# Softmax reciprocals of a fused attention and MoE kernel: 28 of 32 loads issued by SyncE, 14 transposes two steps sooner

## The chip, the cores and the metric

The kernel runs on one NeuronCore of a Trainium2 chip. The core has TensorE (PE, with its weight loads shown apart as PEld), VectorE (DVE), ScalarE (ACT), GpSimd (POOL) and SyncE (SP, which only issues DMAs). Each engine works through its own instructions in order, and engines wait for each other by semaphores. The metric is the device time of one execution in microseconds. The kernel before took 644.96 us, the median of 3 runs (644.65 to 645.30).

## The reference

Three stages in float32. First an attention in which a query sees only the keys of its own cluster, then two feed-forward stages:

```python
mask = q_assign[:, :, :, None] == k_assign[:, :, None, :]      # argmax over 16 centroids
scores = np.where(mask, scale * q @ k.T, -1e9)
scores = scores - np.max(scores, axis=-1, keepdims=True)
attn = np.exp(scores)
attn = attn / (np.sum(attn, axis=-1, keepdims=True) + 1e-09)   # the reciprocals of this case
x = attn @ v                                                   # [2, 8, 768, 64] -> [1536, 512]
x = leaky_relu(x @ w_in) @ w_out                               # 512 -> 2048 -> 512
out = x + gate * expert(x)   where x @ w_skip > 0, one of 8 experts per token, 512 -> 1024 -> 512
```

The inputs are 2 batches of 8 heads with 768 tokens and 64 values a head.

## The kernel before, in words

The attention is a written-out sequence of 96 steps. Two heads make a pair; there are 8 pairs (p = 0 to 7) of 12 steps each (r = 0 to 11). Six steps make a group g (0 to 15): three tiles of 128 queries for two heads. In step s TensorE computes the scores of one query tile against all 768 keys (tile `sps`), VectorE takes the row maximum (`st`), ScalarE takes the exponential with its row sum (`pr`, `sm`). Three steps later (LAG = 3) TensorE transposes the 128x768 exponentials in six pieces (`tps`) and ScalarE copies them to SBUF in two halves (`pt`). In every second step TensorE multiplies them with the values (`avps`, 8 matmuls). At the end of a group ScalarE copies the sum out (`xr`) and GpSimd multiplies it with the reciprocals (`rb`) and splits it into two parts for the next stage (`xh`, `xl`).

The reciprocals take their own way. With rf the step within the six that follow a group: at rf 0 and 1 VectorE adds 1e-9 to the six row sums and inverts them (`rc`); at rf 4 `recip_rows` has TensorE transpose `rc` into PSUM (`rcps`) and ScalarE copy six rows out (`rrow`); at rf 5 SyncE writes them to DRAM (`recip_scratch`); one step later (rf 0 of the next six) GpSimd issues `recip_load`, two DMAs that spread them over 128 partitions (`rb`); at the next rf 2 GpSimd multiplies.

Beside this each pair is prepared during the steps of the pair before. A table (`plan`) names step and slot of each part: slot "a0" comes before the transposes of a step, "pb" at its end. The preparation uses one PSUM buffer, tag "M", of which there is a single one (`ps_m`, bufs=1). For pairs 3 to 7 it holds in turn four transposed pieces of q and k (`rawps`: TensorE at the end of steps 5, 6, 7 and 8, ScalarE reads each in slot "a0" of the step after, tile `raw`), then the centroid scores (`asps`, step 9, read in step 10), their transposes (`scps`, step 10) and in step 2 of the next pair the masks (`ohps`). `rcps` is a tile of the same buffer. In every fourth step ScalarE also starts the conversion of a piece of 64-bit weights (`cvu`).

What a step appends stands in this order in the program: scores, weight conversion, slot "a0", transposes and their copies, `recip_rows`, values, exponential, end of group, `recip_load`, `recip`, slots "d" and "pb". The functions that matter are `recip_rows` (L404), `recip_load` (L411), `raw_act` (L187) and the step loop (L688 on). SyncE issues nearly all other transfers of the stage in the order written: copies between halves (`UA`, `UB`, `VA`, `VB`), masks (`mk`), values, weights (`stg`).

Of the kernel before, what the change touches and what calls it, by code (L numbers as in the profile page):

```python
# [20 lines left out]
def _f(ap):  # L21
    return ap.bitcast(F32)
# [3 lines left out]
def kernel(  # L26
# [14 lines left out]
    nc = tc.nc  # L41
# [17 lines left out]
    def pool(name, side=None, **kw):  # L59
        return tc.alloc_tile_pool(name=name, side=side, bufs=1, reuse_waits="tile", **kw)  # L60
# [8 lines left out]
    def ps_s(name):  # L69
        return psum.tile([P, 2, 512], F32, tag="S", name=name, bufs=2)  # L70
# [281 lines left out]
    NSTEP = B * NPAIR * 12  # L352
# [5 lines left out]
    def where(s):  # L358
        p, r = divmod(s, 12)
        half, r = divmod(r, 6)  # L360
        j, h = divmod(r, 2)
        return p, half, j, h

    def st_scores(s):
        p, half, j, h = where(s)
        U, V = (uv_t[p][h], uv_t[p][2 + h])
        qs = slice((3 * half + j) * P, (3 * half + j + 1) * P)
        ps = ps_s("sps")
        for (t, n), first in (((U, 80), True), ((V, P), False)):
            for kh in range(2):  # L370
                nc.tensor.matmul(ps[:, kh, 0:HS], lhsT=t[0:n, 0, qs], rhs=t[0:n, 1, kh * HS:(kh + 1) * HS],  # L371
                                 start=first, stop=not first)
        st = att.tile([P, 1], F32, tag="st", name="st", bufs=7)
        nc.vector.tensor_reduce(out=st[:, 0:1], in_=ps[:, :, 0:HS], axis=AX.XY, op=ALU.max, negate=True)  # L374
        pr = att.tile([P, 2, HS], F32R, tag="pr", name="pr", bufs=4)
        pr = _f(pr)
        p_t[s] = pr, st
        s_t[s] = ps
# [13 lines left out]
    rc_t, rrow_t = {}, {}  # L392
# [9 lines left out]
    rscr = nc.dram_tensor("recip_scratch", (NSTEP // 6, 6, P), F32, kind="Internal").ap()  # L402

    def recip_rows(g):  # L404
        ps = (ps_t if g == NSTEP // 6 - 1 else ps_m)([P, P], "rcps")
        nc.tensor.transpose(ps, rcs[g % 2], ident)
        row = att.tile([6, P], F32, tag="rrow", name="rrow", bufs=2)
        nc.scalar.activation(out=row, in_=ps[0:6, :], func=AF.Copy)
        rrow_t[g] = row

    def recip_load(g):  # L411
        rb = att.tile([P, HS], F32, tag="rb", name="rb", bufs=1)
        for h in range(2):
            nc.gpsimd.dma_start(rb[64 * h:64 * h + 64, :], rscr[g, 3 * h:3 * h + 3, :].rearrange("j q -> (j q)").partition_broadcast(64))
        rrow_t[g] = rb

    t_t = {}

    def st_transpose(s):
        p, half, j, h = where(s)  # L420
        if j == 0:
            pt_t[p, half, h] = att.tile([P, NT, 3, P], F32, tag=f"pt{h}", name=f"pt{h}", bufs=2)
        pr, _ = p_t.pop(s)
        t_t[s] = []
        for kh in range(2):
            ps = ps_t([P, 3, P], "tps")
            for t in range(3):
                nc.tensor.transpose(ps[:, t, :], pr[:, kh, t * P:(t + 1) * P], ident)  # L428
            t_t[s].append(ps)

    def st_evac(s):
        p, half, j, h = where(s)
        pt = pt_t[p, half, h]
        for kh in range(2):
            nc.scalar.activation(out=pt[:, 3 * kh:3 * kh + 3, j, :], in_=t_t[s][kh], func=AF.Copy)  # L435
        t_t.pop(s)

    def st_av(g, kt):
        p, half = divmod(g, 2)
        if kt == 0:  # L440
            av_t[g] = (ps_m if g == NSTEP // 6 - 1 else ps_a)([P, HS], "avps")
        for h in range(2):
            nc.tensor.matmul(av_t[g][64 * h:64 * h + 64, :], lhsT=vnat[p][:, h, kt, :],  # L443
                             rhs=pt_t[p, half, h][:, kt].rearrange("p j c -> p (j c)"),
                             start=(kt == 0), stop=(kt == NT - 1))
# [3 lines left out]
    def av_evac(g):  # L449
        xr_t[g] = att.tile([P, HS], F32, tag="xr", name="xr")  # L450
        nc.scalar.activation(out=xr_t[g], in_=av_t.pop(g), func=AF.Copy)
# [98 lines left out]
    def load_piece(c, a):  # L550
        if wsp[0] is None or a % 2:
            t = ring_a.tile([P, 512, 2], U32, tag="stg", name="stg", bufs=2)
        else:
            t = wsp[0].tile([P, 512, 2], U32, tag="stg2", name="stg2", bufs=2)
        g, wo = divmod(c, 2)
        if wo == 0:
            src = wi_u[a * P:(a + 1) * P, g * 1024:(g + 1) * 1024]
        else:
            src = wo_u[g * 512 + a * P:g * 512 + (a + 1) * P, :]
        nc.sync.dma_start(t, src.rearrange("p (f two) -> p f two", two=2))  # L560
        stage[c, a] = t
# [3 lines left out]
    def convert_op(c, a, i):  # L565
        st = stage[c, a]
        w0, w1_ = st[:, :, 0], st[:, :, 1]
        V = nc.vector
        if i == 0:
            cv[c, a] = [ring_a.tile([P, 512], U32, tag=n, name=n, bufs=2) for n in ("cvu", "cvt")]  # L570
        u, t = cv[c, a]
        if i == 0:
            nc.scalar.activation(out=_f(u), in_=_f(w1_), func=AF.Abs)
        elif i == 1:
            V.tensor_scalar(out=_f(u), in0=_f(u), scalar1=2.0 ** -15, scalar2=None, op0=ALU.max)
        elif i == 2:
            V.tensor_scalar(out=t, in0=u, scalar1=3, scalar2=0x3FFFFFF8, op0=ALU.logical_shift_left,
                            op1=ALU.bitwise_and)
        elif i == 3:
            V.scalar_tensor_tensor(out=t, in0=w1_, scalar=0xC0000000, in1=t, op0=ALU.bitwise_and, op1=ALU.bitwise_or)  # L580
        else:
            direct = not NDIR <= 4 * c + a < NPC
            if direct and (a == 0 or c not in chunks):
                chunks[c] = alloc_chunk(c)
            o = chunks[c][:, a, :].bitcast(U32) if direct else t
            V.scalar_tensor_tensor(out=o, in0=w0, scalar=29, in1=t, op0=ALU.logical_shift_right, op1=ALU.bitwise_or)
            stage.pop((c, a))
            if direct:
                cv.pop((c, a))
# [23 lines left out]
    def preps(p, r, slot):  # L613
        prep(p + 1, r, slot)
        if r >= 4:
            prep(p + 2, r - 12, slot)
# [3 lines left out]
    def conv_step(s, late):  # L620
        n = 2 * s + late - CONV0
        if s == 6 and not late:
            load_piece(0, 0)
            load_piece(0, 1)
        m, r = divmod(n, CPER)
        if 0 <= m < NPC:
            c, a = divmod(m, 4)
            if r < 5:
                convert_op(c, a, r)
            elif r == 6:  # L630
                if m >= NDIR:
                    nc.sync.dma_start(wf32[c - NDIR // 4, :, a, :], _f(cv.pop((c, a))[1]))
                if m + 2 < NPC:
                    load_piece(*divmod(m + 2, 4))
# [54 lines left out]
    for s in range(NSTEP + 12 + LAG):  # L689
        p, r = divmod(s, 12)  # L690
        if s < NSTEP:
            st_scores(s)
        conv_step(s, 0)
        preps(p, r, "a0")
        preps(p, r, "pa")
        if 0 <= s - LAG < NSTEP:
            st_transpose(s - LAG)
            st_evac(s - LAG)
        gf, rf = divmod(s, 6)
        if 0 < gf <= NSTEP // 6:  # L700
            if rf == 4:
                recip_rows(gf - 1)
            elif rf == 5:
                nc.sync.dma_start(rscr[gf - 1], rrow_t.pop(gf - 1))
        g, kt = divmod(s - 6 - LAG, 6)
        if 0 <= g < NSTEP // 6 and kt % 2:
            st_av(g, kt - 1)
            st_av(g, kt)
        if s < NSTEP:
            st_exp(s)  # L710
        if 0 <= g < NSTEP // 6 and kt == NT - 1:
            av_evac(g)
            av_split(g)
        if 0 <= g < NSTEP // 6 and kt == 3:
            recip_load(g)
        if 0 < gf <= NSTEP // 6 and rf < 2:
            recip(gf - 1, rf)
        preps(p, r, "d")
        preps(p, r, "pb")
        if r == 10 and p + 1 < NP:  # L720
            load_v(p + 1)
        conv_step(s, 1)
        if s == NSTEP:
            att_a.release()
            rt = pool("rt", "left")
            ring_b[0] = pool("ring_b", "left")
            wip[0] = pool("wi", "left")
            for c in range(NDIR // 4, NPC // 4):
                load_f32(c)
            load_next(2)  # L730
        if s == NSTEP + 4:
            for i in range(3):
                split_i(i)
# [891 lines left out]
```

## Time and profile before

| what | value |
|---|---|
| median of 3 runs | 644.96 us (644.65 to 645.30) |
| profiled execution | 644.19 us, its span 642.5 us |
| TensorE busy in the span | 624.0 us, 97% |
| ScalarE, VectorE, GpSimd busy | 65%, 75%, 26% |
| the 96 attention steps | from 18.6 us on; the last values end at 252.6 us |

Times in rows are microseconds from the span's start. In the chain of waits a row gives start, length and what the time went to; consecutive rows join without gaps, so the start of one is the end of the one before. A row of instructions in order of time ends with the idle time of the engine before it and its releaser, in brackets. Matmuls overlap: their ends are modelled.

### The profile page before, as it was taken

Reading aid. Unit: us, or ns where it says so; the run is one execution under the profiler, and the core shown is the slowest. Engines: PE = TensorE matmul, PEld = TensorE weight load, DVE = VectorE, ACT = ScalarE, POOL = GpSimd, SP = SyncE. Lnnn points to the kernel's source line nnn. Section 1 sums busy time; section 2 is a strip of 40 time slices with the busy share of each in tenths; the row PEclk is TensorE's granted clock in tenths of the full one; section 3 lists DMA queues with packets and bytes.
Section 4 is the critical chain, followed back from the end, with each engine's and each line's share of the span. In section 5 each row is a group of like instructions: output and inputs, shape, how many; then the busy total and the mean of one; then the engine's idle time right before and its main releaser. Section 6 shows DMA issues by size and latency. Waiting matters only on the chain.

```text
span 642.5 us, 10035 instructions
## 1 busy us (share of the span) xinstructions
PE 624.0 (97%) x3505; PEld 484.2 (75%) x3505; DVE 484.7 (75%) x893; ACT 417.0 (65%) x817; POOL 164.4 (26%) x215
## 2 busy tenths in 40 slices
PE   5999999999999999999999999999999999999994
PEld 3777777677777775888888888878888778688874
DVE  6757868777878754988865888868887748999961
ACT  5798898988888885655454444435445446688860
POOL 3333647463746333400000000000000125005211
PEclk9999999999999999999999999999999999999998
DMA  7766566578766508132014301008421739999930
GB/s 189 193 180 169 138 153 190 150 197 199 200 186 162 174 31 318 67 119 91 23 36 146 100 33 34 33 2 301 178 94 66 267 137 318 372 363 350 369 135 28
DMA packets 66246, 104.26 MB, mean 162 GB/s; under 512 B 27994, under 2 KB 32060, under 8 KB 65810
## 3 DMA queue, kind: packets, MB, share of 16 engines
q1 hardware_dynamic: 62914, 95.36, 47.5%
q0 software_dynamic: 3280, 8.24, 3.9%
q8 instruction: 28, 0.46, 0.3%
q14 instruction: 24, 0.20, 0.1%
HBM read 77.45 MB, written 12.72 MB: 140 GB/s over the span
## 4 chain that ended last, share of the span: by engine, by line
PE 91%; DVE 3%; ACT 2%; DMA 2%; SPq 1%; issue 1%; POOL 0%; POOLq 0%
PE ups L669 20%; PE acc L775 19%; PE sps L371 10%; PE avps L443 10%; PE tps L428 9%; PE hps L1316 7%; PE yps L1347 7%; PE rawps L179 1%; PE hT L1328 1%; PE acc L1208 1%; PE asps L232 1%; ACT pr L389 1%; DMA stg<-in_moe_w_in_dram 1%; DMA first<-in_k_dram 1%; PE scps L244 1%
## 5 line engine op out<-in xcount | busy, mean ns | idle before, releaser
L374 DVE TENSOR_REDUCE st<-sps 128x1 f32<-128x768 f32 x96 | 91.5, 954 | 49.9 <-PE sps L371 49.1
L435 ACT ACTIVATE pt<-tps 128x384 f32<-128x384 f32 x192 | 85.4, 508 | 17.6 <-PE tps L428 16.4
L389 ACT ACTIVATE pr<-sps,st 128x768 f32<-128x768 f32 x96 | 88.0, 917 | 11.5 <-DVE st L374 11.4
L428 PE MATMUL tps<-ident,pr 128*128 128x128 f32 x576 | 79.0, 273 | 0.5 <-ACT pt L435 0.5
L669 PE MATMUL ups<-xh,whii 128*128 128x512 f32 x192 | 74.9, 390 | 0.0
L669 PE MATMUL ups<-xh,wloi 128*128 128x512 f32 x192 | 74.7, 389 | 0.0
L669 PE MATMUL ups<-xl,whii 128*128 128x512 f32 x192 | 74.7, 389 | 0.0
L428 PEld LDWEIGHTS tps<-ident,pr 128*128 128x128 f32 x576 | 67.9, 140 | 5.6 <-ACT pt L435 1.6
L443 PE MATMUL avps<-pt,vnat 128*64 128x384 f32 x384 | 72.1, 498 | 0.0
L775 PE MATMUL acc<-whio,gh 128*128 128x512 f32 x183 | 72.1, 394 | 0.0
L775 PE MATMUL acc<-whio,gl 128*128 128x512 f32 x183 | 71.3, 389 | 0.0
L775 PE MATMUL acc<-wloo,gh 128*128 128x512 f32 x183 | 71.2, 389 | 0.0
L760 ACT ACTIVATE gh<-g 128x512 fp32r<-128x512 f32 x48 | 30.4, 632 | 47.5 <-DVE g L759 47.5
L758 ACT ACTIVATE lk<-ups 128x512 f32<-128x512 f32 x48 | 28.5, 595 | 48.8 <-PE ups L669 43.4
L762 DVE TENSOR_TENSOR gl<-g,gh 128x512 fp32r<-128x512 f32 x48 | 33.2, 691 | 25.2 <-ACT gh L760 25.2
L1048 POOL DMA_INDIRECT xe<-x_scratch,eix x1 | 1.2, 1165 | 189.8 <-DVE eix L1047 189.8
L881 DVE SCALAR_TENSOR_TENSOR ohe<-x,x2Ts 128x512 f32<-128x512 f32 x63 | 43.4, 689 | 1.5
L443 PEld LDWEIGHTS avps<-pt,vnat 128*64 128x64 f32 x384 | 23.4, 136 | 25.5 <-issue 25.1
L759 DVE TENSOR_TENSOR g<-ups,lk 128x512 f32<-128x512 f32 x48 | 33.0, 688 | 12.7 <-ACT lk L758 12.1
L669 PEld LDWEIGHTS ups<-xh,whii 128*128 128x128 f32 x192 | 36.0, 188 | 8.0 <-issue 0.6
L669 PEld LDWEIGHTS ups<-xh,wloi 128*128 128x128 f32 x192 | 36.0, 188 | 7.5
L669 PEld LDWEIGHTS ups<-xl,whii 128*128 128x128 f32 x192 | 36.1, 188 | 7.4
(312 smaller groups left out, 1367.1 us busy)
## 6 DMA issues: line engine op xcount, KB each, us to landing
rawb<-in_moe_w_dram SPq DMA_DIRECT2D x25, 1024.0 KB
rawa<-in_moe_w_dram SPq DMA_DIRECT2D x10, 1024.0 KB
stg<-in_moe_w_in_dram SPq DMA_DIRECT2D x16, 512.0 KB
stg<-in_moe_w_out_dram SPq DMA_DIRECT2D x16, 512.0 KB
x2Ts<-gate_scratch SPq DMA_DIRECT2D x18, 256.0 KB
UB<-UA SPq DMA_DIRECT2D x16, 192.0 KB
vnat<-in_v_dram SPq DMA_DIRECT2D x8, 384.0 KB
rb<-recip_scratch POOLq DMA_DIRECT2D x32, 96.0 KB, 2.8
```

What stands on the lines that cost most here:

```text
L371: nc.tensor.matmul(ps[:, kh, 0:HS], lhsT=t[0:n, 0, qs], rhs=t[0:n, 1, kh * HS:(kh + 1) * HS], start=first, stop=not first)
L374: nc.vector.tensor_reduce(out=st[:, 0:1], in_=ps[:, :, 0:HS], axis=AX.XY, op=ALU.max, negate=True)
L389: nc.scalar.activation(out=pr, in_=ps[:, :, 0:HS], func=AF.Exp, bias=st[:, 0:1], accum_out=sm_t[g][:, 3 * h + j:3 * h + j + 1])
L428: nc.tensor.transpose(ps[:, t, :], pr[:, kh, t * P:(t + 1) * P], ident)
L435: nc.scalar.activation(out=pt[:, 3 * kh:3 * kh + 3, j, :], in_=t_t[s][kh], func=AF.Copy)
L443: nc.tensor.matmul(av_t[g][64 * h:64 * h + 64, :], lhsT=vnat[p][:, h, kt, :], rhs=pt_t[p, half, h][:, kt].rearrange("p j c -> p (j c)"), s ...
L669: nc.tensor.matmul(ps, lhsT=w[:, cc, :], rhs=x[:, blk, cc, :], start=(n == 0), stop=(n == 3 * KD - 1))
L762: nc.vector.tensor_tensor(out=gl, in0=g, in1=_f(gh), op=ALU.subtract)
L775: nc.tensor.matmul(ps, lhsT=a[:, ts_], rhs=w, start=(fc == 0 and n == 0), stop=(fc == NFC - 1 and n == 2))
L881: nc.vector.scalar_tensor_tensor(out=junk[0].rearrange("p t n -> p (t n)"), in0=x2_t[blk, t // 2][:, t % 2, :], scalar=1.0, in1=wgb_t[blk, ...
L1316: nc.tensor.matmul(ps, lhsT=x[:, c, :], rhs=w, start=(n == 0), stop=(n == len(mm) - 1))
L1347: nc.tensor.matmul(ps[:, cs], lhsT=x[:, f, :], rhs=w[:, cs], start=(h == 0 and f == 0 and n == 0), stop=(h == 1 and f == 3 and n == 2))
```

## The change

`recip_load` takes the engine that issues it, and the write to DRAM becomes a function. For the groups called inner (g = 1 to 14) `recip_rows` moves from rf 4 to rf 2, the write from rf 5 to rf 3, and the load from GpSimd at rf 0 of the next six to SyncE at rf 5. Groups 0 and 15 stay as they were, and so do 4 loads of GpSimd.

```diff
-    def recip_load(g):
+    def recip_load(g, eng):
         rb = att.tile([P, HS], F32, tag="rb", name="rb", bufs=1)
         for h in range(2):
-            nc.gpsimd.dma_start(rb[64 * h:64 * h + 64, :], rscr[g, 3 * h:3 * h + 3, :].rearrange("j q -> (j q)").partition_broadcast(64))
+            eng.dma_start(rb[64 * h:64 * h + 64, :], rscr[g, 3 * h:3 * h + 3, :].rearrange("j q -> (j q)").partition_broadcast(64))
         rrow_t[g] = rb
+
+    def recip_write(g):
+        nc.sync.dma_start(rscr[g], rrow_t.pop(g))
...
+        gf, rf = divmod(s, 6)
+        inner = 1 < gf < NSTEP // 6
+        if inner and rf == 3:
+            recip_write(gf - 1)
+        elif inner and rf == 5:
+            recip_load(gf - 1, nc.sync)
         conv_step(s, 0)
...
-        gf, rf = divmod(s, 6)
         if 0 < gf <= NSTEP // 6:
-            if rf == 4:
+            if rf == (2 if inner else 4):
                 recip_rows(gf - 1)
-            elif rf == 5:
-                nc.sync.dma_start(rscr[gf - 1], rrow_t.pop(gf - 1))
+            elif rf == 5 and not inner:
+                recip_write(gf - 1)
...
-        if 0 <= g < NSTEP // 6 and kt == 3:
-            recip_load(g)
+        if g in (0, NSTEP // 6 - 1) and kt == 3:
+            recip_load(g, nc.gpsimd)
```

On TensorE, steps 7 and 8 of pair 2, before (the row `rawps` is the third piece of the preparation, the two rows `avps` the first of the four of step 8):

```order
230 L179 MATMUL rawps<-ident,natk 128x128 x3
231 L371 MATMUL sps<-UA 128x384 x2
232 L371 MATMUL sps<-VA 128x384 x2
233 L428 MATMUL tps<-ident,pr 128x128 x6
234 L443 MATMUL avps<-pt_907,vnat 64x384
235 L443 MATMUL avps<-pt_936,vnat 64x384
```

The same place in the changed kernel:

```order
230 L179 MATMUL rawps<-ident,natk 128x128 x3
231 L371 MATMUL sps<-UA 128x384 x2
232 L371 MATMUL sps<-VA 128x384 x2
233 L431 MATMUL tps<-ident,pr 128x128 x6
234 L406 MATMUL rcps<-ident,rc_114 128x128
235 L446 MATMUL avps<-pt_912,vnat 64x384
236 L446 MATMUL avps<-pt_941,vnat 64x384
```

`rcps` of group 4 now stands in step 8, behind the third piece and before the values; before it stood in step 10, at row 246, between the transposes and the values of that step.

On SyncE, steps 1 to 5 of a pair, before:

```order
51 L213 DMA UB_771<-UA_770 64x768
52 L215 DMA VB_773<-VA_772 64x768
53 L216 DMA VB_773<-UA_770 64x768
54 L560 DMA stg_1098<-in_moe_w_out_dram 128x1024
55 L213 DMA UB_771<-UA_770 64x768
56 L218 DMA VA_772<-VB_773 64x768
57 L219 DMA VA_772<-UA_770 64x768
58 L224 DMA VA_772<-UA_770 64x768
59 L704 DMA recip_scratch<-rrow_1144 6x128
60 L226 DMA VB_773<-UB_771 64x768
61 L310 DMA UA_770<-mk_1117 16x384 x4
```

The same place in the changed kernel:

```order
53 L213 DMA UB_774<-UA_773 64x768
54 L215 DMA VB_776<-VA_775 64x768
55 L216 DMA VB_776<-UA_773 64x768
56 L418 DMA recip_scratch<-rrow_1078 6x128
57 L563 DMA stg_1103<-in_moe_w_out_dram 128x1024
58 L213 DMA UB_774<-UA_773 64x768
59 L218 DMA VA_775<-VB_776 64x768
60 L219 DMA VA_775<-UA_773 64x768
61 L224 DMA VA_775<-UA_773 64x768
62 L414 DMA rb_1162<-recip_scratch 64x384 x2
63 L226 DMA VB_776<-UB_774 64x768
```

The write went five places forward, and two loads stand where it was, ahead of the last copy between halves and the eight masks.

## Rows read from the trace of the kernel before

**Rows 1.** The page, part 1: busy us, share, instructions.

```profile
PE 624.0 (97%) x3505; PEld 484.2 (75%) x3505; DVE 484.7 (75%) x893; ACT 417.0 (65%) x817; POOL 164.4 (26%) x215
```

**Rows 2.** Stretches: busy PE, PEld, DVE, ACT, POOL, granted clock, DMA share, GB/s.

```profile
20.00:40.00 20.00, 18.72 (x124) 14.77 (x124) 13.10 (x19) 17.30 (x42) 2.97 (x4) 1.00 0.65 176
120.00:140.00 20.00, 20.00 (x137) 14.38 (x136) 15.05 (x25) 17.60 (x42) 10.49 (x15) 1.00 0.58 162
...
630.00:642.00 12.00, 4.26 (x36) 4.06 (x34) 1.50 (x3) 0.00 (x0) 1.97 (x2) 0.80 0.10 36
```

**Rows 3.** Chain of waits, 100 to 128 us: start, us, what.

```profile
106.87 1.44 PE avps L443 x8
...
121.43 1.44 PE avps L443 x8
...
127.07 0.11 PE rcps L406
```

**Rows 4.** ACT in order of time, 119 to 122 us: start, us, instruction.

```profile
119.45 0.87 ACT L435 ACTIVATE pt<-tps 128x384 f32<-128x384 f32 x2 [0.55 <-PE tps L428]
...
121.08 0.73 ACT L573 ACTIVATE cvu<-stg 128x512 f32<-128x512 f32 x1
121.66 0.54 ACT L191 ACTIVATE raw<-rawps 128x384 f32<-128x384 f32 x1
```

**Rows 5.** Chain of waits, step 8 of pairs 1, 2, 4 and 5.

```profile
62.81 1.44 PE avps L443 x7
...
92.13 1.44 PE avps L443 x8
...
150.47 1.44 PE avps L443 x8
...
179.61 1.44 PE avps L443 x8
```

**Rows 6.** ACT in order of time, the third piece in the same steps.

```profile
63.04 0.48 ACT L191 ACTIVATE raw<-rawps 128x384 f32<-128x384 f32 x1
...
92.36 0.54 ACT L191 ACTIVATE raw<-rawps 128x384 f32<-128x384 f32 x1
...
150.65 0.52 ACT L191 ACTIVATE raw<-rawps 128x384 f32<-128x384 f32 x1
...
179.70 0.53 ACT L191 ACTIVATE raw<-rawps 128x384 f32<-128x384 f32 x1
```

**Rows 7.** Chain of waits, step 10 of pair 0 (group 0).

```profile
36.50 0.39 ACT raw L191
...
36.93 0.33 PE rcps L406
```

**Rows 8.** Chain of waits, step 4 of pair 1 (group 1).

```profile
51.97 0.57 DVE eq L256
...
52.58 0.33 PE rcps L406
```

**Rows 9.** DVE in order of time, step 1 of pair 3.

```profile
106.27 0.17 DVE L400 RECIPROCAL rc<-sm 128x6 f32<-128x6 f32 x1
```

**Rows 10.** Who waited for whom, 40 to 262 us: total us, times, longest.

```profile
POOL rb L414 <- DMA recip_scratch<-rrow: 47.4, 13, 6.0
...
POOL xr L457 <- DMA rb<-recip_scratch: 7.1, 3, 2.6
```

**Rows 11.** Chain of waits, 211 to 220 us.

```profile
212.28 5.14 DMA stg<-in_moe_w_in_dram
...
218.27 0.86 ACT pt L435 x2
```

**Rows 12.** The DRAM scratch: ns of an issue (min/median/max), and us to landing.

```profile
L414 POOL DMA_DIRECT2D rb<-recip_scratch x32: 522/554/782, 43.3 to 255.1; - x32
L704 SPq DMA_DIRECT2D recip_scratch<-rrow x16: 277/337/687, 39.9 to 249.2; - x16
...
DMA to landing us min/median/max: 2.6/2.8/7.3
```

## The prediction

> **What bounds the kernel now.** I read the busy shares first, then the busy time by stretch, then the chain of waits through the attention stage, and last ScalarE in order of time at the places where the change puts something in. The busy shares show TensorE at 97% and no other engine above 75% [rows 1]. By stretch, TensorE is busy 20.00 of 20.00 us at 120 to 140 us, with ScalarE next at 17.60 and GpSimd at 10.49 [rows 2]; the granted clock there is 1.00, the upper level of 2.4 GHz. In the chain of waits from about 54 us to 204 us nothing appears but pieces of TensorE, one behind the other. So in the part that the change touches a microsecond in which TensorE stands still is a microsecond of the kernel, and time saved on any other engine is worth nothing unless TensorE waited for it.
>
> GpSimd does wait, and long: 47.4 us in 13 waits for the write of the reciprocals to land [rows 10]. But who waits for GpSimd's loads in turn is GpSimd itself, 7.1 us in 3 waits before its multiply [rows 10], and no wait of TensorE for either is in the trace. The change removes waiting that the end of the kernel never saw.
>
> **The change part by part.** *The loads leave GpSimd.* That takes 28 issues of 0.554 us median, 15.5 us, from GpSimd [rows 12], an engine busy half the time [rows 2], and most of the 47.4 us of waiting. GpSimd's splits of the next pair come about two issues, 1.1 us, sooner where a load stood among them. On the path: 0, since TensorE's work covers it.
>
> *The loads arrive on SyncE.* There 28 issues come in, at 0.337 us by the median of its own small write, 0.554 us by GpSimd's, 0.687 us by its longest [rows 12]; I take 0.55. For a pair that is four issues, 2.2 us. They stand ahead of the last copy between halves and the eight masks. Behind the loads wait in step 5 these copies, which the scores of the next pair need seven steps later, and in step 11 a piece of weights. The loads themselves wait for the write, issued two steps earlier: with 29.3 us a pair (121.43 - 92.13 [rows 3, 5]) two steps are 4.9 us, and with a landing like the loads' 2.6 to 2.8 us [rows 12] it is there. The one place where SyncE is already late is pair 6: a piece of weights issued at 212.28 lands 5.14 us later and ScalarE's copies at 218.27 follow from it [rows 11], which the chain then carries into TensorE. There the write leaves its place and two loads come in, between 2 x 0.337 - 0.687 = 0 and 2 x 0.687 - 0.337 = 1.0 us more; against that the splits come sooner by up to 1.1 us. I take 0, and keep -0.3 to +1.0 for the range.
>
> *The loads share SyncE's queue.* A load issued by GpSimd landed in 2.8 us, at worst 7.3 us [rows 12]. The Trainium skill, in "DMA: Bandwidth & Descriptors", section Terms, says that on each DMA engine descriptors are consumed in ring order; a load in step 11 would then stand behind the keys, queries and values of the next pair. No run here shows it yet. By that rule, with three transfers of 384 KB at the 162 to 176 GB/s of this stage [rows 2], it would land about 1.2 MB / 0.17 = 7 us after its issue, an estimate, and just about when GpSimd multiplies, three steps on. The sum stands without these sentences: a late `rb` holds GpSimd only, and the bound from rows is the 7.3 us above, against the same three steps. Cost 0.
>
> *The transposes move from rf 4 to rf 2.* Each is one matmul that takes 0.11 us in the chain when it waits for nothing [rows 3]; there are as many as before, and at both places one stands between transposes and a batch of values. So the work moves at no cost, and what counts is whether its two inputs are ready two steps sooner.
>
> First the reciprocals. In step 1 of pair 3 VectorE inverts at 106.27 to 106.44 [rows 9], and the transposes of step 2, behind which `rcps` would now start, end at 106.87 [rows 3]. 0.43 us remain. Cost 0, thinly covered. What reads the buffer next is the masks in step 2 or the fourth piece in step 8; both come behind the 1.44 us of values [rows 3], in which ScalarE copies `rrow`. Cost 0.
>
> Second the PSUM buffer. There is one buffer of tag M, and `rcps` needs it free. In step 2 of pairs 2 to 7 its last user was read in step 11. In step 8 it is not free: the third piece of the next-but-none pair's q and k was put there at the end of step 7, and ScalarE reads it in slot "a0" of step 8. With pair 3 as the example: the transposes of step 8 end at 121.43, where today the values follow at once [rows 3]; ScalarE reads the third piece at 121.66 to 122.20, behind the weight conversion at 121.08 [rows 4]. Today nobody minds, since the fourth piece comes only after the values. In the changed kernel `rcps` stands before the values and must wait for 122.20, and TensorE, in order, waits with it.
>
> The trace has one such wait already: in step 10 of pair 0 ScalarE's read ends at 36.50 + 0.39 = 36.89, `rcps` follows at 36.93 and takes 0.33 instead of 0.11 [rows 7, 3]. So one stall costs (end of the read - end of the transposes) + 0.04 + 0.33 - 0.11 = the difference + 0.26. The five places (pairs 1 to 5; pair 0 keeps its old place, pairs 6 and 7 prepare nothing in these steps):
>
> - pair 1: 63.52 - 62.81 = 0.71, with 0.26 it is 0.97 [rows 5, 6]
> - pair 2: 92.90 - 92.13 = 0.77, so 1.03 [rows 5, 6]
> - pair 3: 122.20 - 121.43 = 0.77, so 1.03 [rows 3, 4]
> - pair 4: 151.17 - 150.47 = 0.70, so 0.96 [rows 5, 6]
> - pair 5: 180.23 - 179.61 = 0.62, so 0.88 [rows 5, 6]
>
> Together 4.87 us. Is there anything behind each that takes it back? TensorE ran without a gap before and after, so a later wait that would have swallowed it is not there. Would ScalarE come sooner? Its queue in step 7 starts with a wait of 0.55 us for TensorE's transposes [rows 4], so it is in time with TensorE there, and the `rrow` copy taken out of step 4 moves nothing.
>
> One wait goes: for group 1 `rcps` stood in step 4 behind VectorE's reading of the same buffer, until 52.54, and took 0.33 instead of 0.11 [rows 8]. In step 2 it finds the buffer read in time. Gain 0.22.
>
> *The sum.* 4.87 - 0.22 = 4.65 us. On the profiled execution, 644.19 us with its span of 642.5, that is 648.8. The median shown is 0.77 above the profiled execution, so the median after is 644.96 + 4.65 = 649.6.
>
> **The rivals.** *A, the buffer is read in time.* If ScalarE finished the third piece about 1 us sooner, before the transposes end, the stalls vanish and the 0.22 and the 0.3 that I keep for the late weights of pair 6 remain as gains: 644.4, not slower. It decides in step 8: the read must end before the transposes do. For it: the spread of the difference, 0.62 to 0.77, is small, and 0.73 us of conversion stand before it [rows 4], so any order with the read first would do. Against it: the change touches nothing on ScalarE between the wait of 0.55 us and the read. Half-way, with 0.3 to 0.5 a stall, it would be 646.2 to 647.2.
>
> *B, GpSimd's waiting mattered after all.* 47.4 us of waiting and 15.5 us of issuing leave GpSimd; if GpSimd's splits gated the scores of the next pair, its issue of one load, 0.55 us, would come back at each of 7 changes of pairs, 3.9 us: it nearly cancels the stalls, or ends at 641.1 without them. Against it: TensorE has no gap at any change of pairs from 54 us on.
>
> *C, SyncE becomes a bound.* Its 2.2 us a pair and the loads' waits push the masks or the weights past the step that needs them, in pairs 4 to 7 at 0.3 to 1.0 us each, on top of the stalls: 650.8 to 653.6. For it: pair 6 [rows 11]. Against it: only one piece of weights was late.
>
> *D, the clock.* With TensorE idle for 1.28 of 20 us between 20 and 40 us the granted clock stayed at 1.00 there, the upper level; it is 0.80 at 630 to 642 us, where TensorE works 4.26 of 12 us [rows 2]. The Trainium skill, "TensorE: Matmul & The Clock Gate", section "A second HAM failure mode: psum-queue depth-cycling", says that short idling between groups of matmuls can make the clock swing. By that rule the trace's 20 to 40 us would show a fall, and it does not. Priced from rows: 0.80 over 12 us is 4.8 us at the lower level of 1.2 GHz, which loses 2.4 us of work; five times 12 us, 661.
>
> **How the numbers follow.** Forecast (five stalls, 3.3 to 5.9 us after the other terms): 0.69, its own range 648.3 to 650.9. Rival A in full 0.10, half-way 0.09. B 0.05, of which 0.01 cancels the stalls. C 0.06, D 0.01. A measurement of this kernel can tell about 0.2%, 1.3 us, from no change. Slower than 646.3: forecast, 0.07 of half-way, C, D: 0.83. Within 643.7 to 646.3: A, the rest of half-way and 0.01 of B, 0.13. Faster: the rest of B, 0.04. The range for 8 in 10 leaves out A in full, B, D and most of C: 646.2 to 651.2.
>
> **What would show it.** Right: in step 8 of pairs 1 to 5 TensorE idle 0.6 to 0.9 us before `rcps`, released by ScalarE's `raw`, and no such idle time in steps 2 or in pairs 6 and 7; the chain of waits passing through `raw` five times; GpSimd's waits for `recip_scratch` down to those of groups 0 and 15; everything after 190 us later by about 4.7 us and otherwise alike. Wrong: `rcps` following the transposes at once in step 8, which makes it A; gaps of TensorE at the start of a pair, released by a DMA, which makes it C; a granted clock below 1.00 in the stage, which makes it D; or waits of `rcps` for VectorE in step 2, where I left 0.3 us.

## The result, and the profile after

The changed kernel takes 649.69 us (median of 4 runs, 648.57 to 650.96). The kernel before took 644.81 beside it (4 runs, 644.27 to 645.3): ratio 1.0077, interval 1.0056 to 1.0097. It is 4.88 us slower; the forecast was 4.65.

The profiled execution took 649.46 us with a span of 647.8, which is 5.28 more than the span before. I put the pieces of TensorE of both traces side by side, step by step, and noted where the distance between them grew:

| where | later, us |
|---|---|
| step 8 of pairs 1 to 5, in front of `rcps` (1.02, 1.08, 1.08, 1.07, 1.08), less the 0.11 that `rcps` no longer takes in step 10 | 4.78 |
| step 4 of pairs 2 to 6, in front of the scores (0.34, 0.39, 0.68, 0.68, 0.39) | 2.48 |
| pair 1, steps 4 and 6 (-0.42, +0.51) | 0.09 |
| the two feed-forward stages, to the end of the last matmul (0.33 of it at one place of the first) | 0.35 |
| from the last matmul to the end of the span (8.2 before, 5.8 after) | -2.42 |
| sum | 5.28 |

Shifts of less than 0.2 us are left out; with the start of the attention, 0.13 earlier here, they add up to nothing. The first line is the forecast's main term. The second and the last were not in it, and they nearly cancel. So the total came out right with two of its terms missing. (In the table the matmul of 0.11 us that moved from step 4 to step 2 of pairs 2 to 6 is taken as no shift.)

The 0.33 us of the feed-forward stage stand at 269.14. There the chain of waits of the changed kernel (start, us, what) runs through VectorE, which splits weights for that stage and so comes late to `g`, an input of TensorE; the kernel before has nothing but TensorE there.

```profile
267.06 1.43 DVE wloi L649
268.48 0.61 DVE g L767
...
269.14 2.33 PE acc L783 x9
```

The page's busy times answer to [rows 1]: little work has gone, and TensorE's share is a point lower.

```profile
PE 624.5 (96%) x3505; PEld 482.8 (75%) x3505; DVE 480.6 (74%) x893; ACT 418.0 (65%) x817; POOL 147.6 (23%) x187
```

By stretch, the same 20 us as in [rows 2] (columns as there). TensorE has 0.75 us of idle time where it had none, and the granted clock is 1.00, the upper level.

```profile
120.00:140.00 20.00, 19.25 (x132) 13.93 (x130) 12.93 (x22) 16.77 (x40) 7.86 (x11) 1.00 0.67 182
```

TensorE in order of time in the changed kernel, `rcps` in step 8 of pairs 1 to 5 (start, us, instruction, in brackets the idle time before it and who ended it). In front of each TensorE stands idle for 0.70 to 0.76 us until ScalarE has read the third piece, and the transpose takes 0.33 us. No other `rcps` of these pairs waits for anything, and the chain of waits passes through `raw` in front of each of the five.

```profile
63.59 0.33 PE L406 MATMUL rcps<-ident,rc 128*128 128x128 f32 x1 [0.70 <-ACT raw L191]
...
94.23 0.33 PE L406 MATMUL rcps<-ident,rc 128*128 128x128 f32 x1 [0.76 <-ACT raw L191]
...
124.87 0.33 PE L406 MATMUL rcps<-ident,rc 128*128 128x128 f32 x1 [0.75 <-ACT raw L191]
...
155.51 0.33 PE L406 MATMUL rcps<-ident,rc 128*128 128x128 f32 x1 [0.75 <-ACT raw L191]
...
186.16 0.33 PE L406 MATMUL rcps<-ident,rc 128*128 128x128 f32 x1 [0.76 <-ACT raw L191]
```

ScalarE in the changed kernel in step 8 of pair 3 has the order of [rows 4], all 2.7 us later: the wait of 0.55 us, the weight conversion, then the read, which ends at 124.81. `rcps` follows at 124.87.

```profile
122.14 0.87 ACT L438 ACTIVATE pt<-tps 128x384 f32<-128x384 f32 x2 [0.55 <-PE tps L431]
...
123.77 0.67 ACT L576 ACTIVATE cvu<-stg 128x512 f32<-128x512 f32 x1
124.32 0.49 ACT L191 ACTIVATE raw<-rawps 128x384 f32<-128x384 f32 x1
```

Who waited for whom in the changed kernel, 40 to 267 us (total us, times, longest). GpSimd's 47.4 us in 13 waits [rows 10] are down to 4.5 in one. TensorE has two lines that it did not have: the stalls, and 2.0 us of its scores for ScalarE's exponential.

```profile
POOL rb L414 <- DMA recip_scratch<-rrow: 4.5, 1, 4.5
...
PE rcps L406 <- ACT raw L191: 3.7, 5, 0.8
PE sps L371 <- ACT pr L389: 2.0, 6, 0.4
```

The last of these lines leads to the term that I had not foreseen. The chain of waits of the changed kernel in steps 1 to 4 of pair 2 (start, us, what) runs through VectorE and ScalarE, where before it was all TensorE:

```profile
77.94 1.18 DVE oh L269
79.12 1.00 DVE cvt L583
80.11 0.87 DVE st L374
...
81.07 0.07 ACT pr L389
81.14 0.73 issue
81.87 0.20 ACT pr L389
82.07 0.04 issue
82.12 0.96 PE sps L371 x4
```

VectorE's comparison `oh` has become long, the row maxima `st` come late, so does the exponential, and TensorE's scores in step 4 wait 0.35 us for it, in each of five pairs. The comparison by its tile, 70 to 205 us (ns of one, min/median/max), in the kernel before, and below it in the changed kernel: same operation, same shape, 2.4 times as long by the median.

```profile
L269 DVE TENSOR_TENSOR oh<-eq,mx x5: 510/517/761, 76.9 to 193.8; 128x384 bf16<-128x384 f32 x5
```

```profile
L269 DVE TENSOR_TENSOR oh<-eq,mx x5: 1255/1257/1262, 77.9 to 200.4; 128x384 bf16<-128x384 f32 x5
```

What GpSimd does at that moment differs. Before, in pair 4, it issues its two loads from 136.46 to 137.56, and its split comes later. `oh` ran at 135.50, while GpSimd sat waiting for the write:

```profile
136.46 1.10 POOL L414 DMA_DIRECT2D rb<-recip_scratch  x2 [1.74 <-DMA recip_scratch<-rrow]
137.59 0.93 POOL L208 TENSOR_SCALAR UA<-raw 128x384 fp32r<-128x384 f32 x1
```

In the changed kernel GpSimd has neither loads nor wait there. Its subtraction (line 209) runs from 138.93 to 139.99, and VectorE's `oh` from 139.14 to 140.40, GpSimd first and then VectorE:

```profile
138.93 1.06 POOL L209 TENSOR_TENSOR VA<-raw,UA 128x384 fp32r<-128x384 f32 x1
139.96 0.81 POOL L208 TENSOR_SCALAR UA<-raw 128x384 fp32r<-128x384 f32 x1
```

```profile
139.14 1.26 DVE L269 TENSOR_TENSOR oh<-eq,mx 128x384 bf16<-128x384 f32 x1
140.32 1.08 DVE L583 SCALAR_TENSOR_TENSOR cvt<-stg,cvt 128x512 uint32<-128x512 uint32 x1
```

In pairs 2, 3 and 6 the kernel before was not undisturbed either: there the operation behind `oh` (`cvt`) took 1.13 to 1.16 us beside GpSimd's splits, against 0.75 in pairs 4 and 5. So the changed kernel loses 0.34 to 0.39 us in those three pairs and 0.68 in the other two.

Taken alone the rows show only that the two lie beside each other. The Trainium skill, "SBUF — State Buffer", section "Who interferes with whom", says that a VectorE instruction with two SBUF inputs contends with a GpSimd instruction that reads SBUF. Both are of that kind here, and the trace agrees: 0.52 us without the subtraction beside it, 1.26 with it. Whether the one makes the other is what the kernel with the filler, below, tries.

The rows also tell how much it is. Of the 1.06 us of the subtraction 0.21 are over when `oh` begins; 0.85 are left, and `oh` ends 0.41 behind them: 0.85 + 0.41 = 1.26, in all five pairs within 0.01. It matters which of the two began first. In the kernel with the order alone GpSimd's line 208, which reads SBUF too, begins 0.14 us behind `oh` and runs beside the rest of it, and `oh` keeps its 0.51:

```profile
139.11 0.74 POOL L208 TENSOR_SCALAR UA<-raw 128x384 fp32r<-128x384 f32 x1
```

```profile
138.97 0.51 DVE L269 TENSOR_TENSOR oh<-eq,mx 128x384 bf16<-128x384 f32 x1
```

This is read from the rows; no kernel was made to try it.

The last term is the end of the program. The span and the last matmul of the kernel before, then of the changed kernel: from 634.27 to 642.5 are 8.2 us, from 641.96 to 647.8 only 5.8.

```profile
core 0: 642.5 us, clock 0.996
...
633.99 0.28 PE L1347 MATMUL yps<-phi,hTl 128*128 128x256 f32 x1
```

```profile
core 0: 647.8 us, clock 0.999
...
641.68 0.28 PE L1355 MATMUL yps<-phi,hTl 128*128 128x256 f32 x1
```

In both the write of the last output is issued 0.8 us behind the end of that matmul. What got shorter is how GpSimd's queue closes: in the trace's records an update of its DMA semaphores and a drain take 1.26 and 4.40 us before, 0.71 and 2.83 after, 2.12 of the 2.42 us. GpSimd issues 53 DMAs in the kernel before (32 loads and 21 others) and 25 in the changed one.

### The profile page after: what moved, and what is told of

Same layout as the page of the kernel before. It is cut to its first block, busy times and chain, and to the rows that moved or that the text cites. A ratio compares the mean times of both kernels' runs of the same rounds, so it can differ in the third digit from the quotient of the medians.

```text
span 647.8 us, 10032 instructions
## 1 busy us (share of the span) xinstructions
PE 624.5 (96%) x3505; PEld 482.8 (75%) x3505; DVE 480.6 (74%) x893; ACT 418.0 (65%) x817; POOL 147.6 (23%) x187
## 4 chain that ended last, share of the span: by engine, by line
PE 81%; DVE 6%; ACT 5%; DMA 4%; issue 2%; POOL 1%; SPq 1%; POOLq 0%; ACTq 0%; DVEq 0%
PE ups L672 19%; PE acc L783 18%; PE sps L371 8%; PE avps L446 8%; PE hps L1324 7%; PE yps L1355 7%; PE tps L431 6%; ACT pr L389 2%; DVE st L374 2%; PE rawps L179 1%; PE hT L1336 1%; PE acc L1216 1%; DVE oh L269 1%; ACT pt L438 1%; DMA VB<-VA 1%
```

## The experiments

Theory T, set up from the two traces before any of these kernels was measured: the change is three things, stalls in step 8 that come from the order alone, a collision of `oh` with GpSimd's split that comes from the loads leaving GpSimd alone, and a shorter end that comes from the number of GpSimd's DMAs alone. Rivals: the stalls come from the loads on SyncE; all of the loss is in the order, and the loads are worth nothing.

What was measured (medians; the kernel before took 644.81 beside the changed one, 644.71 beside the next four and 645.2 beside the last three, 23 runs each for these two; idle and `oh` by the profiles):

| kernel | median | ratio, interval | idle before `rcps`, step 8 | `oh` | idle before scores, step 4 | tail |
|---|---|---|---|---|---|---|
| changed | 649.69 | 1.0077, 1.0056 to 1.0097 | 0.70 to 0.76 | 1.26 | 5 x 0.35 | 5.8 |
| loads only | 647.47 | 1.0053, 1.0036 to 1.0069 | none | 1.26, once 0.75 | 4 x 0.45, 0.52 | 5.8 |
| order only | 649.94 | 1.0084, 1.0067 to 1.0102 | 0.70 to 0.76 | 0.51 | none | 8.2 |
| changed + filler | 646.38 | 1.0024, 1.0015 to 1.0033 | 0.70 to 0.75 | 0.52 | none | 5.7 |
| loads + filler | 647.05 | 1.0036, 1.0025 to 1.0048 | none | 0.52 | none | 5.6 |
| read first | 646.42 | 1.0024, 1.0013 to 1.0035 | 0.15 to 0.20 | 1.26 | 5 x 0.35 | 5.8 |
| odd groups | 646.65 | 1.0020, 1.0007 to 1.0034 | none | 0.51, once 0.82 | none | 7.0 |
| read first + filler | 643.88 | 0.9982, 0.9973 to 0.9991 | 0.15 to 0.20 | 0.52 | none | 5.8 |

**The loads alone.** SyncE issues the 28 loads, but at the old place, and the transposes and the write stay where they were (against the kernel before; `recip_load` takes the engine as in the change):

```diff
         if 0 <= g < NSTEP // 6 and kt == 3:
-            recip_load(g)
+            recip_load(g, nc.sync if 0 < g < NSTEP // 6 - 1 else nc.gpsimd)
```

> SyncE issues the 28 loads, transposes, writes and loads stand where they stood before the change. Theory T (three terms: five stalls of TensorE before rcps in step 8, +4.8 us; GpSimd's splits, which come 1.1 us or more sooner without the loads, meet VectorE's one-hot operation (oh) in step 1 and delay it by 0.75 us, which costs TensorE 0.35 to 0.7 us at five changes of pairs, +2.5 us; GpSimd's drain at the end of the program is shorter by 2.4 us with 28 fewer loads of its own): no stall, so attention ends 2.5 us later, the tail is 2.4 us shorter, about 645. Theory R (the recorded sum: stalls only): attention ends as before, the tail as before, 644.8.

It took 647.47 us. No stall in step 8, `oh` at 1.26 in four pairs, the short tail: these three came as T has it, so the stalls do not come from SyncE's loads, and the collision needs no change of order. The time did not come: it is 2.8 us above before. T had left out SyncE. SyncE's queue waited, 40 to 262 us (total, times, longest):

```profile
SPq L414 <- DMA recip_scratch<-rrow: 29.3, 9, 5.5
```

In the old order the load of an even group stands close behind its write, and where GpSimd had waited for the write to land, SyncE does now. But these waits are not what TensorE felt. The chain of waits of this kernel at the end of pair 6 (start, us, what) goes through a piece of weights:

```profile
217.25 5.85 DMA stg<-in_moe_w_in_dram
223.10 0.02 issue
223.13 0.03 ACT cvu L576
```

In front of it on SyncE stand the two loads of an odd group, whose write had been issued at 208.04. They waited for nothing and took 1.89 us to issue:

```profile
214.69 1.89 SPq L414 DMA_DIRECT2D rb<-recip_scratch  x2
...
217.25 0.43 SPq L563 DMA_DIRECT2D stg<-in_moe_w_in_dram  x1
```

ScalarE waits 2.65 us for this piece, and TensorE's transposes 1.51 us for ScalarE; step 1 of pair 7 is 1.78 us later for it. The loads of another odd group stand in front of a piece at the start of pair 6 in the same way (185.07 to 186.30, the piece issued at 187.53, landed 5.88 us later); ScalarE waits 1.24 us for it, and steps 1 and 2 are 0.98 us later. Step 4 of pair 6 is 0.56 us later with a wait of the scores for ScalarE's exponential of 0.52, the fifth behind `oh`. So by the rows SyncE became a bound through the time that the loads' issues take right in front of weights, and not through the waits for the write; no kernel tries the one without the other. In the changed kernel, where the loads stand ahead of the masks, SyncE's wait for the write is 5.8 us in 4, and no weights are late by more than 0.6.

**The order alone.** The transposes and the write as in the changed kernel, all loads with GpSimd at their old place:

```diff
-        elif inner and rf == 5:
-            recip_load(gf - 1, nc.sync)
...
-        if g in (0, NSTEP // 6 - 1) and kt == 3:
+        if 0 <= g < NSTEP // 6 and kt == 3:
             recip_load(g, nc.gpsimd)
```

> Transposes at rf 2 and writes at rf 3 as in the change, but GpSimd issues all 32 loads at their old place. T: five stalls, no meeting of the splits with oh (oh 0.5 us as before), tail as before: +4.7 us, 649.5. R: the same 649.4. Both fall if the time is back at 644.8.

It took 649.94 us. TensorE's waits, 55 to 215 us, are those of the changed kernel to a tenth, and there is no wait of the scores:

```profile
PE rcps L406 <- ACT raw L191: 3.7, 5, 0.8
```

`oh` is back at 0.51 us, the tail at 8.2 us. So the five stalls belong to the order, and collision and short tail both belong to the loads. A further 1.19 us came from a late piece of weights at the end of pair 6 (a gap of 0.91 us), the place of [rows 11]. SyncE carries no loads there, so weights can be late at this place without them.

**A filler in the place of the loads.** The changed kernel, in which GpSimd writes an already used constant tile six times (1.76 us) where its loads stood; nothing reads that tile afterwards:

```diff
+        if 0 < g < NSTEP // 6 - 1 and kt == 3:
+            for _ in range(6):
+                nc.gpsimd.memset(cexp, 0.0)
```

> The changed kernel, and GpSimd clears a dead constant six times (about 1 us, which adds work and changes no result) where it issued the loads before. T: the splits are back at their old times, oh runs 0.5 us, no gap of TensorE in step 2; the stalls in step 8 and the short tail stay: 649.7 - 2.5 = 647.2. R, and any theory in which SyncE's two loads cause the late steps: 649.7.

It took 646.38 us, 3.3 less than the changed kernel, by giving an engine work that is of no use. GpSimd in pair 4 of this kernel, and below it VectorE: `oh` now runs while GpSimd only writes, and the subtraction comes behind it.

```profile
137.29 1.76 POOL L726 MEMSET cexp<- 128x128 f32 x6
...
139.71 1.00 POOL L209 TENSOR_TENSOR VA<-raw,UA 128x384 fp32r<-128x384 f32 x1
```

```profile
138.13 0.52 DVE L269 TENSOR_TENSOR oh<-eq,mx 128x384 bf16<-128x384 f32 x1
```

The five waits of the scores are gone and the five stalls remain, at 0.70 to 0.75 us. So the collision is a question of what GpSimd does beside `oh`, and it is shown. In step 4 of pairs 2 to 6 the changed kernel lost 2.48 us against the kernel before; this one gains 0.92 there (0.34, 0.29 and 0.29 in pairs 2, 3 and 6, where the kernel before had its scores late as well, with no idle time to show it). The difference, 3.4 us, agrees with that of the two medians, 649.69 - 646.38 = 3.3.

**The loads alone, with the filler.** The first kernel with the filler of the third.

> e1_loads_only with the same filler on GpSimd: loads on SyncE, transposes in their old place. T: no stalls, no meeting with oh, the tail 2.4 us shorter: 642.4, faster than both kernels. R: 644.8.

It took 647.05 us, and T failed here by 4.7. `oh` is short, nothing stalls in step 8, the tail is 5.6; but SyncE waits 30.3 us in 9, ScalarE 3.25 us for the weights of pair 6, and TensorE 2.12 us for ScalarE, which is 2.4 us of delay; another 1.9 us went in pairs 5 and 6. The kernel repeats what the first one had shown: at the end of pair 6 the two loads, 2.06 us of issue without a wait, stand in front of the late weights. With this the loads could not be priced apart from the order.

**The read first.** The changed kernel, with ScalarE's read of the third piece ahead of the weight conversion in step 8:

```diff
-        conv_step(s, 0)
-        preps(p, r, "a0")
+        if r == 8:
+            preps(p, r, "a0")
+            conv_step(s, 0)
+        else:
+            conv_step(s, 0)
+            preps(p, r, "a0")
```

> The changed kernel, and in step 8 ScalarE reads the third piece ahead of the weight conversion instead of behind it (0.73 us sooner); nothing else moves. T: rcps finds the buffer free about 0.7 us sooner, five gaps of 0.75 us shrink to 0.1 us or less, about 3.5 us gone; the meetings with oh and the short tail stay: 646.2. If rcps waits for something else than this read: 649.7.

It took 646.42 us, ScalarE and TensorE in step 8 of pair 3 (the same columns):

```profile
122.72 0.50 ACT L191 ACTIVATE raw<-rawps 128x384 f32<-128x384 f32 x1
123.09 0.68 ACT L576 ACTIVATE cvu<-stg 128x512 f32<-128x512 f32 x1
```

```profile
123.27 0.33 PE L406 MATMUL rcps<-ident,rc 128*128 128x128 f32 x1 [0.20 <-ACT raw L191]
```

The wait is down from 0.75 to 0.20 us (T had 0.1 or less) and the step's delay from 1.08 to 0.53, five times over; `oh` and the waits of the scores are untouched. This takes away the suspected cause alone, and three quarters of each wait go with it: most of a stall is the conversion that stands ahead of the read. Five times 0.55 are 2.7 us; the two ratios stand 3.4 us apart, with intervals of about 1 us on both.

**Every second group.** The change made for the odd inner groups only; the even ones keep order, write and GpSimd's loads. The load on GpSimd then stays where `oh` would collide, and no `rcps` comes to step 8:

```diff
-        inner = 1 < gf < NSTEP // 6
+        inner = 1 < gf < NSTEP // 6 and gf % 2 == 0
...
-        if g in (0, NSTEP // 6 - 1) and kt == 3:
+        if (g % 2 == 0 or g == NSTEP // 6 - 1) and 0 <= g < NSTEP // 6 and kt == 3:
             recip_load(g, nc.gpsimd)
```

> The change for the seven odd groups only (transposes in step 2, loads on SyncE); the even groups, whose transposes would stall in step 8 and whose loads on GpSimd keep the splits behind oh, as before the change. T: no stall, oh 0.5 us, 14 DMAs of GpSimd fewer: after the last matmul 7.0 us instead of 8.2 (5.8 with 28 fewer): 643.5. If the tail does not go by the number of GpSimd's DMAs: 8.2 or 5.8 us there. R: 644.5.

It took 646.65 us. The tail is what T had worked out for 39 DMAs; the span and last matmul of this kernel:

```profile
core 0: 645.5 us, clock 0.994
...
638.20 0.28 PE L1355 MATMUL yps<-phi,hTl 128*128 128x256 f32 x1
```

With 53, 39 and 25 DMAs of GpSimd the tail is 8.2, 7.0 and 5.8 us, in steps as even as the counts: 2.42 / 28 = 0.086 us for each. All the DMAs that went are of one kind, loads of `rb`. Stalls and collisions are gone too. What T missed is in pair 5, first on GpSimd, then on ScalarE, then on TensorE:

```profile
167.85 1.10 POOL L414 DMA_DIRECT2D rb<-recip_scratch  x2 [3.70 <-DMA recip_scratch<-rrow]
...
177.87 0.49 ACT L191 ACTIVATE raw<-rawps 128x384 f32<-128x384 f32 x1 [2.94 <-POOL VB L209]
...
178.41 0.55 PE L179 MATMUL rawps<-ident,natq 128*128 128x128 f32 x3 [1.82 <-ACT raw L191]
```

GpSimd waits for a write, everything behind it is late, its split `VB` ends at 177.83, ScalarE's read needs that buffer, and TensorE the piece after. Steps 6 to 8 of this pair are 3.4 us later (1.89, 0.54 and 0.99), and without these the time would be 643.2, where T had 643.5. Before, the same wait of ScalarE was 0.39 us at the most and TensorE did not see it. So GpSimd's waiting can reach TensorE; in the kernel before it was covered, with little to spare.

**The read first, with the filler.** Both remedies on the changed kernel; by the medians this one is 0.2% faster than the kernel before:

> e4_filler and the read ahead of the conversion in step 8: both added waits of TensorE taken away, the loads on SyncE and the early order kept. T: 646.4 - 3.5 = 642.9, faster than the kernel before by the shorter tail. If stalls and meetings are not all of it: 644 to 646.

It took 643.88 us against 645.2, ratio 0.9982 (0.9973 to 0.9991). Its row on TensorE in step 8 of pair 3 is

```profile
121.28 0.33 PE L406 MATMUL rcps<-ident,rc 128*128 128x128 f32 x1 [0.20 <-ACT raw L191]
```

By the profile its attention stage is still 2.35 us longer than before, counted from its own start: 5 x 0.53 - 0.55 = 2.10 for the stalls that are left, 0.26 in pair 1, 0.88 for late weights at the end of pair 6, less the 0.92 in step 4; the rest nearly cancels. The 2.4 us of the shorter tail pay for that, 0.27 more are lost in the first feed-forward stage, and the attention starts 0.87 us earlier in this execution than in the one of before. The same start differs by -0.87 to +0.81 us from one profiled execution to another, so I do not count it as a gain; without it the two traces differ by +0.2 us, where the medians differ by -1.3. That this kernel is faster rests on the medians alone, and where the gain comes from the two traces do not show. T had 642.9 and missed by 1.0, about the size of the late weights.

## Why the prediction was right

The time, 649.69 for a forecast of 649.6, came out for the reason given in its largest term, and stayed there because two terms that it did not have, +2.48 and -2.42, are of opposite sign. That part of the fit is luck. Step by step:

- *Five stalls of `rcps` in step 8, 4.87 us.* Right in place, cause and size: 1.02 to 1.08 each, 4.78 net by the trace. Two runs bear it out from both sides: the order alone brings the same five waits, the read put first takes three quarters of each away. One stall was given as the difference + 0.26; measured, 0.75 of idle goes with 1.08 of delay, 0.97 without the 0.11 that it no longer takes in step 10.
- *The loads leave GpSimd, on the path 0.* This step failed. The prediction had seen that the splits come 1.1 us sooner, and counted that as harmless since TensorE's work covers GpSimd. It did not ask what stands on another engine at the time to which they move. VectorE's `oh` did, and 2.48 us came of it; the filler shows it.
- *Nothing said of the end of the program.* The prediction counted each of the 28 loads by its issue and its landing, and looked no further than the attention stage. The end shrank by 2.42 us with 28 DMAs of GpSimd fewer, and by 1.24 with 14 fewer.
- *The loads arrive on SyncE, 0.* Right for this change: an issue took 0.587 us by the median for the 0.55 taken, and the gap of TensorE behind the late weights of pair 6 grew from 0.11 to 0.20. That the write would be there after two steps failed 4 times, 5.8 us of waiting in all, at no cost seen on TensorE. In both kernels with the loads alone rival C is seen at the end of pair 6, at 1.8 to 2.4 us; there the loads stand right in front of the weights.
- *The loads share SyncE's queue, 0.* Right as far as the trace tells: it has the landing of five of the 28 loads, 4.6 us at worst, where GpSimd's had 7.3 [rows 12], and no multiply of GpSimd waited for any of them. Three of the five were issued in step 11; they landed in 2.8 to 4.6 us, not in the 7 that the prediction had estimated by the rule on ring order. The Trainium skill, "DMA: Bandwidth & Descriptors", has that rule in the section "Queues, rings and completion order". The changed kernel's scratch transfers (columns as there; the landings are those of five loads of SyncE and two of GpSimd):

```profile
L414 SPq DMA_DIRECT2D rb<-recip_scratch x28: 450/587/918, 56.0 to 246.0; - x28
...
DMA to landing us min/median/max: 2.8/3.3/4.6
```

- *The reciprocals are ready two steps sooner; masks and fourth piece are covered.* Right: no `rcps` waited for VectorE in step 2, and no matmul for `rrow`.
- *Group 1, a gain of 0.22.* The gain in step 4 was there, 0.42, of which the moved matmul takes 0.11 in step 2; the remaining 0.31 are the 0.22 and an idle time of 0.09 that the prediction left out. 0.51 was lost again in steps 6 and 7, at gaps of TensorE of 0.21 us for ScalarE's copies `pt` and of 0.14 for VectorE's masks `mk`. The order alone loses 0.41 there and the loads alone nothing, so this too belongs to the order; what made the two late is open.
- *Rival B.* GpSimd's waiting did not show in the changed kernel, but the run with every second group has the path that it describes. The reason given against it, that TensorE has no gap at any change of pairs, holds for the kernel as it was, but for 0.11 us in step 2 of pair 7, and says nothing on how far it is from one.
- *The clock.* With five idle times of 0.75 us and five of 0.35 us the granted clock was 1.00 in each stretch of 20 to 25 us from 60 to 205 us.

Of what was to be seen "right" and "wrong": the stalls, their releaser and GpSimd's waits were as named, and steps 2 and pairs 6 and 7 had no such idle time. "Everything after 190 us later by about 4.7 us" was not: it is 7.35 later at the end of attention.

Open are why `pt` and `mk` come late in pair 1, why the weights at the end of pair 6 are late by such different times (TensorE loses between 0 and 2.4 us there over the kernels), and where the last kernel's gain comes from.

## What to carry to other kernels

When work is taken off an engine that is not the bound, what stood behind it moves forward: look up, in order of time, what each other engine does in the stretch to which it moves, above all VectorE's operations with two SBUF inputs beside GpSimd's, and which of the two begins first. Where issues go to another queue, look for what stands right behind them there. When an instruction on the bound engine moves ahead, look for the last reader of its buffer and for what stands ahead of that reader on its own engine; a difference of two rows gave the price here within 2%. And compare the ends of the programs, from the last useful instruction to the end of the span, before a total that fits is taken for a confirmed sum.

## What the runs showed of the hardware that was not expected

- The end of the program depends on how many DMAs GpSimd issued in it: 8.2 us from the last matmul to the end with 53, 7.0 with 39, 5.8 with 25 (8.2 and 53 again with the order alone). The DMAs that differ are all loads of `rb`.
- A VectorE comparison of 128x384 with two SBUF inputs takes 0.52 us alone and beside GpSimd's fills, and 1.26 us when GpSimd's subtraction began 0.21 us before it. Beside a one-input operation of GpSimd that begins 0.14 us after it, it keeps 0.51 us.
- An issue of the same load takes about as long on SyncE, 0.587 us, as on GpSimd, 0.554 [rows 12]; with the loads alone SyncE waited 29.3 us for the writes, where GpSimd had waited 47.4 before.
- A wait of TensorE costs more than the idle time that the profile gives it (with ends that are modelled): 0.75 us of idle came with 1.08 of delay, 0.35 with up to 0.68, 0.20 with 0.53, 1.51 with 1.78, some 0.3 on top each time.
